# Left-over keys of a pooled attention: matmuls of 64 rows on two row halves in place of 128 rows, with a new order of issue

## The chip, the cores and the metric

One core of a Trainium2 chip. The metric is the device time of one execution in microseconds (us). The engines are TensorE (matmul, PE in the rows; its weight loads are PEld), VectorE (DVE), ScalarE (ACT), GpSimd (POOL) and SyncE (SP), which issues the DMAs.

## What is computed

Attention with pooled keys and values feeds two chained products with a normalisation between them. Batch 8, 8 heads, 576 queries, head size 64; keys and values are averaged in groups of 8, so 72 keys are left per head.

```python
k_p = k.reshape(B, H, 72, 8, D).mean(axis=3);  v_p likewise
scores = q @ k_p^T / sqrt(D);  attn = softmax(scores)
x = attn @ v_p                        # 4608 rows of 512
h = x @ w_in;  solu = h * softmax(h);  ln = layernorm(solu) * g_ln
x2 = ln @ w_out                       # 512 wide
out = ((x2 @ w1) * (x2 @ w2)) @ w3 @ w_out2
```

## The kernel before

**Split numbers.** Products that need more than one pass of the reduced float type keep a number as a high part (a rounded copy, made by ScalarE) and a low part (the difference, made by VectorE); `split` (L217 to L219) makes both. A product is then high x high, high x low and low x high.

**Units and slots.** The attention is cut into 16 groups of queries (class `Group`), two for each of the 8 batches: the even group has 256 queries, the odd one 256 and the 64 that are left over (320). While group a is in attention, the rows of earlier groups run through `h` (L753, against `w_in`) and `x` (L847 to L849, against `w_out`). Python events are laid out over time slots, 16 for each group, and build the program; behind that, `issue_order` reorders each engine's instructions by `ISSUE_ORDER`, a table in which a number skips forward or back in the engine's list and ":n" takes n of them.

**Main and left-over keys.** Of the 72 pooled keys of a head 64 are main keys and 8 are left over (KM = 64, KL = 8). For the main keys two heads share the 128 rows of a matmul: `pth` and `ptl` are the transposed probabilities' high and low parts, `VBDh` and `VBDl` the values in block-diagonal form. The left-over keys of all 8 heads, 8 x 8 = 64, are put in one tile: `normalize` writes them twice (L665), `pt` transposes them (L686) into `px`, ScalarE copies all 128 rows to `ptx` (L691), and VectorE subtracts on rows 64 to 127 (L695), so that `ptx` has the high parts on rows 0 to 63 and the low parts on rows 64 to 127. `spread_v` makes the weights for it: `vlh` (L553) holds the high left-over v on all 128 rows, masked so that a row counts for its own head only; `VLL` (L554) holds the low part on rows 0 to 63 and zeros below. `load_vl` fetches the left-over v twice, once for each 64 rows (two DMAs, L449).

**The value product.** `Group.av(i)` (L722) is called twice for each group, for the head pairs 2i and 2i + 1. For each pair five matmuls of 128 rows and 128 weight columns add up in one bank: `pth` x `VBDh`, `ptl` x `VBDh`, `pth` x `VBDl`, `ptx` x `vlh`, `ptx` x `VLL`. In even groups (256 columns) the two pairs of a call share one bank and one `split` reads both; in odd groups (320 columns) each pair has a bank, a `split` of its own and a copy-out of the 64 left-over queries (L729). Banks of the kind "ba" are three; scores (L617, two for each tile of queries) and transposed probabilities (L683) use the same three.

**At the start.** `pool_k_first` (L488) pools the first keys with matmuls whose weights have 64 columns: they write partitions 0 to 63 of a bank, then 64 to 127. L348 to L350 (the low part of `w_in`) follow on TensorE.

Of the kernel before, what the change touches and what calls it, by code (L numbers as in the profile page):

```python
# [8 lines left out]
F32 = mybir.dt.float32  # L9
# [16 lines left out]
    ),  # L26
    "Activation": (
# [20 lines left out]
    ),  # L48
    "DVE": (
# [31 lines left out]
    ),  # L81
    "Pool": (
# [9 lines left out]
    ),  # L92
# [38 lines left out]
def attention_moe_kernel(  # L131
# [286 lines left out]
    def heads(t, n):  # L418
        return t.rearrange("p (o d) -> p o d", o=1).to_broadcast([n, H, D])
# [9 lines left out]
    class Batch:  # L429
# [27 lines left out]
        def load_kl(self):  # L457
            self.load_left(KL8, k, 1)
# [1090 lines left out]
```

## Time and profile before

| | before |
|---|---|
| median of 3 runs | 1182.35 us (1180.24 to 1184.98) |
| profiled execution | 1189.81 us, of which the span from the first to the last instruction is 1188.0 us |
| granted TensorE clock, mean | 0.993 of full speed |
| busy: TensorE, VectorE | 1154.3 us (97%), 930.3 us (78%) |
| busy: ScalarE, GpSimd | 540.8 us (46%), 528.1 us (44%) |

Busy time of TensorE is that of overlapping records: a matmul's record is longer than the step to the next one, so a price of a matmul is read from starts in a timeline, and whether TensorE was held up from its waits.

### The profile page before, as it was taken

The numbers are of one execution on the slowest core, as the hardware profiler recorded it, in microseconds if no ns is written. First come the engines' busy times: TensorE is split into PE (matmuls) and PEld (weight loads), VectorE is DVE, ScalarE is ACT, GpSimd is POOL, SyncE is SP. The second block draws the span as 40 slices with busy tenths as digits, with TensorE's granted clock in tenths as the row PEclk, the third lists the DMA queues.
The fourth block names the chain that finished last, engine by engine and source line by source line (L and its number), as shares of the span: only waits on it lengthen the run. The fifth ranks groups of instructions, "written<-read, shape, count | busy, mean of one in ns | idle before, by whom it ended". The sixth has DMA issues, their size and how long they took to land.

```text
span 1188.0 us, 20236 instructions
## 1 busy us (share of the span) xinstructions
PE 1154.3 (97%) x7218; PEld 1034.6 (87%) x7218; DVE 930.3 (78%) x1376; ACT 540.8 (46%) x1399; POOL 528.1 (44%) x482
## 2 busy tenths in 40 slices
PE   7999998999999999999999999999999989999998
PEld 5788887998999999989989888888888868999998
DVE  6899898988676765686658869889785677999972
ACT  4665647575656565555422112131130145454542
POOL 2554655554232321100066757686652263555520
PEclk9999999999999999999989999999999999999999
DMA  9576586968474722355253625536441362354501
GB/s 256 139 141 150 152 208 189 238 202 209 130 174 129 172 90 90 132 190 193 81 162 115 208 94 183 187 124 195 134 142 54 118 246 72 108 184 137 177 37 72
DMA packets 167205, 178.56 MB, mean 150 GB/s; under 512 B 82624, under 2 KB 107200, under 8 KB 167104
## 3 DMA queue, kind: packets, MB, share of 16 engines
q1 hardware_dynamic: 167104, 177.26, 50.9%
q8 instruction: 57, 0.93, 0.3%
q14 instruction: 44, 0.36, 0.1%
HBM read 114.30 MB, written 62.91 MB: 149 GB/s over the span
## 4 chain that ended last, share of the span: by engine, by line
PE 78%; DVE 8%; DMA 6%; ACT 2%; SPq 2%; issue 2%; POOL 1%; ACTq 0%; DVEq 0%; POOLq 0%
PE h L753 12%; PE p L1152 10%; PE p L1154 10%; PE p L1153 10%; PE o L1392 5%; PE o L1390 5%; PE o L1391 5%; PE x L848 4%; PE x L849 4%; PE x L847 4%; PE av L722 3%; PE sc L617 2%; DMA vl<-in_v_dram 1%; PE ow L1313 1%; DMA kv<-in_k_dram 1%
## 5 line engine op out<-in xcount | busy, mean ns | idle before, releaser
L847 PE MATMUL x<-lnh,gwh 128*128 128x256 f32 x576 | 165.6, 288 | 2.3 <-ACT lnh L823 2.0
L849 PE MATMUL x<-lnh,gwl 128*128 128x256 f32 x576 | 163.6, 284 | 1.1 <-DVE gwl L376 1.0
L848 PE MATMUL x<-lnl,gwh 128*128 128x256 f32 x576 | 163.2, 283 | 0.4 <-DVE lnl L824 0.4
L847 PEld LDWEIGHTS x<-lnh,gwh 128*128 128x128 f32 x576 | 109.2, 190 | 3.6 <-ACT lnh L823 2.2
L849 PEld LDWEIGHTS x<-lnh,gwl 128*128 128x128 f32 x576 | 109.0, 189 | 1.7 <-DVE gwl L376 1.7
L848 PEld LDWEIGHTS x<-lnl,gwh 128*128 128x128 f32 x576 | 108.8, 189 | 1.5 <-DVE lnl L824 0.7
L638 ACT ACTIVATE ea<-sc,mx 128x72 f32<-128x72 f32 x320 | 98.4, 327 | 24.8 <-DVE mx L635 24.4
L658 POOL TENSOR_TENSOR pr<-ea,sm 128x512 f32<-128x512 f32 x40 | 42.5, 1062 | 141.5 <-DVE sm L654 84.1
L1168 POOL TENSOR_TENSOR a<-a,b 128x512 f32<-128x512 f32 (+1 forms) x40 | 51.5, 1286 | 109.3 <-issue 67.8
L1156 ACT ACTIVATE p<-p 128x512 f32<-128x512 f32 (+1 forms) x40 | 22.1, 552 | 163.0 <-PE p L1154 144.8
L753 PE MATMUL h<-winh,xh 128*128 128x512 f32 x288 | 94.5, 409 | 1.1 <-DVE e L768 1.1
L753 PE MATMUL h<-winl,xh 128*128 128x512 f32 x288 | 90.7, 394 | 0.0
L753 PE MATMUL h<-winh,xl 128*128 128x512 f32 x288 | 90.1, 393 | 0.0
L638 ACT ACTIVATION_READ_ACCUMULATOR ea<-sc,mx 128x1 f32 x320 | 68.3, 214 | 0.0
L762 ACT ACTIVATE e<-h,ST 128x1024 f32<-128x1024 f32 x36 | 40.2, 1116 | 57.0 <-DVE ST L761 56.7
L753 PEld LDWEIGHTS h<-winh,xl 128*128 128x128 f32 x288 | 54.0, 188 | 11.8
L753 PEld LDWEIGHTS h<-winl,xh 128*128 128x128 f32 x288 | 54.0, 188 | 11.7
L1153 PE MATMUL p<-th,w1h 128*128 128x512 f32 (+1 forms) x160 | 59.1, 370 | 0.0
L1152 PE MATMUL p<-th,w1h 128*128 128x512 f32 (+1 forms) x160 | 59.1, 369 | 0.0
L1154 PE MATMUL p<-th,w1l 128*128 128x512 f32 (+1 forms) x160 | 59.1, 369 | 0.0
L768 DVE SCALAR_TENSOR_TENSOR e<-h,e 128x1024 f32<-128x1024 f32 x36 | 44.0, 1222 | 17.5 <-ACT e L762 17.3
L753 PEld LDWEIGHTS h<-winh,xh 128*128 128x128 f32 x288 | 50.4, 191 | 7.8 <-issue 1.3
(281 smaller groups left out, 3831.5 us busy)
## 6 DMA issues: line engine op xcount, KB each, us to landing
raw<-pd SPq DMA_DIRECT2D x18, 1024.0 KB
pd<-a SPq DMA_DIRECT2D x64, 256.0 KB
ed<-turn SPq DMA_DIRECT2D x28, 512.0 KB
back<-ed SPq DMA_DIRECT2D x112, 128.0 KB
x2d<-xo SPq DMA_DIRECT2D x35, 256.0 KB
kv<-in_k_dram SPq DMA_DIRECT2D x32, 256.0 KB
kv<-in_v_dram SPq DMA_DIRECT2D x32, 256.0 KB
f<-in_moe_w_dram SPq DMA_DIRECT2D x16, 512.0 KB
```

Source lines behind the costliest of these rows:

```text
L638: nc.scalar.activation(e[0:n, x], half[a][:, h], AF.Exp, bias=mx[0:n, x : x + 1], scale=1.0, accum_out=sm[0:n, x : x + 1],)
L753: nc.tensor.matmul(self.ph[:, a], s_[:, c], w_[:, c, a * 512 : a * 512 + 512], start=first, stop=last)
L847: nc.tensor.matmul(o, gw[0][:, f, ws], self.th[:, f], start=(f == 0), stop=False)
L848: nc.tensor.matmul(o, gw[0][:, f, ws], self.tl[:, f], start=False, stop=False)
L849: nc.tensor.matmul(o, gw[1][:, f, ws], self.th[:, f], start=False, stop=(f == FC - 1))
L1152: nc.tensor.matmul(o, wh[:, c, fsl], th[:, c], start=c == 0, stop=False)
L1153: nc.tensor.matmul(o, wh[:, c, fsl], tl[:, c], start=False, stop=False)
L1154: nc.tensor.matmul(o, wl[:, c, fsl], th[:, c], start=False, stop=c == 1)
L1168: nc.gpsimd.tensor_tensor(a[:, 0], a[:, 0], b[:, 0], ALU.mult)
L1390: nc.tensor.matmul(o[:, t], h[:, c, ts], wh, start=(c == 0), stop=False)
L1391: nc.tensor.matmul(o[:, t], h[:, c, ts], wl, start=False, stop=False)
L1392: nc.tensor.matmul(o[:, t], l[:, c, ts], wh, start=False, stop=(c == 3))
```

## The change

Heads 0 to 3 of the left-over keys move to rows 0 to 63 of `ptx`, heads 4 to 7 to rows 64 to 127; in each half 32 rows hold high parts and 32 low parts (high, low, low, high from the top). `vlh` and `VLL` shrink from 8 to 4 heads of columns, since a head's row half picks it out. A call `av(i)` now works on pairs i and i + 2, one from each half, each with a bank of its own: first the three main terms of both pairs (128 rows), then `vlh` and `VLL`, each as two neighbouring matmuls of 64 rows on the two row halves. In even groups both banks are kept over both calls (columns 0 to 255 for i = 0, 256 to 511 for i = 1) and split behind the second. The low part of `ptx` now takes two VectorE instructions of 32 rows instead of one of 64, 40 more in all. `load_vl` issues three DMAs (32, 64 and 32 rows), 8 more in all. `sh` and `sl` have 128 rows, not 64. The fill of `VLL` with zeros goes, a second small mask comes. The order table is new for every engine; a gap of 352 bytes in the last stage's memory goes.

```diff
-    mask8 = const.tile([P, H], F32, tag="mask8", name="mask8")
+    masks = const.tile([P, 2, 4], F32, tag="masks", name="masks")
+    mask4, high4 = masks[:, 0], masks[:, 1]
...
-    nc.vector.tensor_tensor(mask8, m16[:, 0:8], m16[:, 8:16], ALU.add)
+    nc.vector.tensor_reduce(mask4, m16.rearrange("p (t i) -> p i t", i=4), axis=AX.X, op=ALU.add)
+    nc.vector.tensor_tensor(high4, m16[:, 0:4], m16[:, 12:16], ALU.add)
...
-    VLL = A1.tile([P, H, D], F32R, tag="VLL", name="VLL")
-    nc.gpsimd.memset(VLL.bitcast(F32), 0.0)
+    VLL = A1.tile([P, 4, D], F32R, tag="VLL", name="VLL")
...
-            self.load_left(self.vn, v, 2)
+            self.load_left(self.vn, v, ((0, 4, 0), (0, H, 32), (4, 4, 96)))
...
-            self.vlh = A.tile([P, H, D], F32R, tag="vlh", name=f"vlh{self.b}", bufs=1)
-            nc.gpsimd.tensor_tensor(self.vlh, heads(self.vn[:, 0:D], P), head_mask(P), ALU.mult)
-            nc.gpsimd.tensor_tensor(VLL[0:64], heads(sl, 64), head_mask(64), ALU.mult)
+            sh = A.tile([P, D], F32R, tag="sh", name=f"sh{self.b}", bufs=1)
+            sl = A.tile([P, D], F32, tag="sl", name=f"sl{self.b}", bufs=1)
+            split(sh, sl, self.vn[:, 0:D])
+            self.vlh = A.tile([P, 4, D], F32R, tag="vlh", name=f"vlh{self.b}", bufs=1)
+            nc.gpsimd.tensor_tensor(self.vlh, heads(self.vn[:, 0:D]), head_mask(mask4), ALU.mult)
+            nc.gpsimd.tensor_tensor(VLL, heads(sl), head_mask(high4), ALU.mult)
...
+            left = pr[0:n, H * KM :].rearrange("p (a s x) -> p a s x", a=2, s=2)
             for c in range(2):
                 nc.gpsimd.tensor_tensor(
-                    pr[0:n, (H + c) * KM : (H + c) * KM + KM].rearrange("p (h k) -> p h k", h=H),
-                    e[0:n, :, KM:KP],
-                    s8.to_broadcast([n, H, KL]),
+                    left[:, :, c].rearrange("p a (h k) -> p a h k", k=KL),
+                    e[0:n, :, KM:KP].rearrange("p (a h) k -> p a h k", a=2),
+                    s8.rearrange("p (a h) o -> p a h o", a=2).to_broadcast([n, 2, 4, KL]),
                     ALU.mult,
                 )
...
-                nc.vector.tensor_tensor(x[64:P], px[64:P], x[64:P].bitcast(F32), ALU.subtract)
+                for r in (32, 64):
+                    nc.vector.tensor_tensor(x[r : r + 32], px[r : r + 32], x[r : r + 32].bitcast(F32), ALU.subtract)
...
-            for p in (2 * i, 2 * i + 1):
-                if self.g or p % 2 == 0:
-                    av_bank = bank(f"av{self.a}_{p}")
...
+            if self.g or i == 0:
+                self.ab = [bank(f"av{self.a}_{i}_{a}") for a in range(2)]
+            off = 0 if self.g else i * U
+            av = [t[:, off : off + w] for t in self.ab]
+            for a in range(2):
+                p = 2 * a + i
+                vh, vl = [t[:, p].rearrange("p a d -> p (a d)") for t in (VBDh, VBDl)]
+                for n, (l, r) in enumerate(((vh, self.pth), (vh, self.ptl), (vl, self.pth))):
+                    nc.tensor.matmul(av[a], l, r[:, p, 0:w], start=(n == 0), stop=False)
+            for l in (bt.vlh, VLL):
+                for a in range(2):
+                    ks = slice(64 * a, 64 * a + 64)
+                    vp = l[ks, 2 * i : 2 * i + 2].rearrange("p j d -> p (j d)")
+                    nc.tensor.matmul(av[a], vp, self.ptx[ks, 0:w], start=False, stop=l is VLL)
+            for a in range(2):
+                c = 2 * a + i
+                if self.g:
+                    split(x[0][:, c], x[1][:, c], av[a][:, 0:U])
...
+                elif i:
+                    cs = slice(2 * a, 2 * a + 2)
+                    split(x[0][:, cs], x[1][:, cs], self.ab[a].rearrange("p (c n) -> p c n", c=2))
...
-    gap(RB, 352)
```

In the new list of TensorE, one group with 256 columns and its surroundings read, written out (F: a main term of 128 rows; H: a matmul of 64 rows):

```
x (12 matmuls of another unit), F F F F F F, H H H H, scores of the next tile (first half), h x 8, scores (second half), h ...
```

## Rows read from the trace of the kernel before

**Rows 1.** The page: span, busy time, and the chain that ended last by engine.

```profile
span 1188.0 us, 20236 instructions
...
PE 1154.3 (97%) x7218; PEld 1034.6 (87%) x7218; DVE 930.3 (78%) x1376; ACT 540.8 (46%) x1399; POOL 528.1 (44%) x482
...
PE 78%; DVE 8%; DMA 6%; ACT 2%; SPq 2%; issue 2%; POOL 1%; ACTq 0%; DVEq 0%; POOLq 0%
```

**Rows 2.** Busy time of each engine in two stages of the attention.

```profile
core 0: us, PE busy (x) PEld busy (x) DVE busy (x) ACT busy (x) POOL busy (x), PEclk, DMA share, GB/s
50.00:250.00 200.00, 191.72 (x1246) 172.19 (x1245) 179.18 (x330) 127.51 (x459) 109.16 (x143) 0.99 0.72 176
250.00:510.00 260.00, 258.46 (x1747) 238.75 (x1747) 183.53 (x325) 158.84 (x531) 78.07 (x114) 1.00 0.53 148
```

**Rows 3.** All waits of TensorE's matmuls, 250 to 510 us: total, times, longest.

```profile
PE pt L683 <- POOL pr L658: 1.5, 3, 1.0
```

**Rows 4.** Left-over terms of `av`, L722: ns min/median/max, first and last start, forms.

```profile
L722 PE MATMUL av<-ptx,vlh x64: 274/297/468, 43.8 to 498.2; 128*128 128x256 f32 x32, 128*128 128x320 f32 x32
L722 PE MATMUL av<-ptx,VLL x64: 278/304/468, 45.0 to 498.4; 128*128 128x256 f32 x32, 128*128 128x320 f32 x32
```

**Rows 5.** Timeline of TensorE around three calls of `av`: start us, us, instructions.

```profile
401.10 0.27 PE L722 MATMUL av<-pth,VBDh 128*128 128x256 f32 x1
...
402.28 0.28 PE L847 MATMUL x<-lnh,gwh 128*128 128x256 f32 x1
...
404.89 1.14 PE L617 MATMUL sc<-bdt,qT 128*128 128x144 f32 x8
406.34 0.62 PE L753 MATMUL h<-winl,xh 128*128 128x512 f32 x2
406.80 0.63 PE L753 MATMUL h<-winh,xl 128*128 128x512 f32 x2
...
437.38 0.31 PE L722 MATMUL av<-pth,VBDh 128*128 128x320 f32 x1
...
438.84 0.62 PE L753 MATMUL h<-winh,xh 128*128 128x512 f32 x2
```

**Rows 6.** Timeline of TensorE while the first keys are pooled (64 weight columns).

```profile
10.52 0.82 PE L488 MATMUL pkm<-ident,kv 128*64 128x128 f32 x9
...
13.25 0.82 PE L488 MATMUL pkm<-ident,kv 128*64 128x128 f32 x6
```

**Rows 7.** Timeline where the pooling ends, with VectorE and the weight loads.

```profile
12.91 0.83 DVE L338 SCALAR_TENSOR_TENSOR cvb<-f,cvb 128x512 int32<-128x512 int32 x1
...
14.00 0.30 PEld L348 LDWEIGHTS w<-cvb,ident 128*128 128x128 f32 x2 [0.17 <-issue]
```

**Rows 8.** VectorE's subtraction on `ptx`: all of it, and from 50 to 250 us.

```profile
L695 DVE TENSOR_TENSOR ptx<-px,ptx x40: 227/294/296, 29.9 to 488.2; 64x128 fp32r<-64x128 f32 x32, 64x64 fp32r<-64x64 f32 x8
...
50.00:250.00 200.00, 4.81 (x17) 0.99 0.72 176
```

**Rows 9.** Timeline of ScalarE and VectorE behind two calls of `av`.

```profile
404.87 1.04 ACT L823 ACTIVATE lnh<-back 128x1024 fp32r<-128x1024 f32 x1
405.82 0.58 ACT L218 ACTIVATE xh<-av 128x512 fp32r<-128x512 f32 x1
406.51 0.68 DVE L219 TENSOR_TENSOR xl<-av,xh 128x512 fp32r<-128x512 f32 x1
...
438.31 0.38 ACT L218 ACTIVATE xh<-av 128x256 fp32r<-128x256 f32 x1 [0.81 <-PE av L722]
438.72 0.42 DVE L219 TENSOR_TENSOR xl<-av,xh 128x256 fp32r<-128x256 f32 x1 [0.71 <-ACT xh L218]
439.06 0.22 DVE L729 COPY X<-av 128x64 f32<-128x64 f32 x1
```

**Rows 10.** GpSimd's product into `vlh` and the DMAs of the left-over v.

```profile
L553 POOL TENSOR_TENSOR vlh<-vl,mask x8: 1042/1042/1373, 38.5 to 441.8; 128x512 fp32r<-128x512 f32 x8
...
L449 SPq DMA_DIRECT2D vl<-in_v_dram x16: 614/628/644, 19.6 to 387.4; - x16
```

More of the change, by code (lines that the diff above doesn't have):

```diff
@@ L416, in attention_moe_kernel, with heads, head_mask @@
     nc.gpsimd.memset(KL8[64:P, 2 * D : 4 * D], 0.0)
-    def heads(t, n):
-        return t.rearrange("p (o d) -> p o d", o=1).to_broadcast([n, H, D])
-    def head_mask(n):
-        return mask8[0:n].rearrange("p (h o) -> p h o", o=1).to_broadcast([n, H, D])
+    def heads(t):
+        return t.rearrange("p (o d) -> p o d", o=1).to_broadcast([P, 4, D])
+    def head_mask(t):
+        return t.rearrange("p (h o) -> p h o", o=1).to_broadcast([P, 4, D])
     def tree(t, n):
@@ L445, in load_main, with load_left @@
             to[i] = t
-        def load_left(self, t, src, copies):
-            for c in range(copies):
+        def load_left(self, t, src, places):
+            for h, n, r in places:
                 nc.sync.dma_start(
-                    t[64 * c : 64 * c + 64], src[self.b, :, 512:S, :].rearrange("h (k e) d -> h k (e d)", e=POOL)
+                    t[r : r + 8 * n], src[self.b, h : h + n, 512:S, :].rearrange("h (k e) d -> h k (e d)", e=POOL)
                 )
@@ L457, in load_kl @@
         def load_kl(self):
-            self.load_left(KL8, k, 1)
+            self.load_left(KL8, k, ((0, H, 0),))
         def load_v(self, i):
@@ L547, in spread_v @@
         def spread_v(self):
-            sh = A.tile([64, D], F32R, tag="sh", name=f"sh{self.b}", bufs=1)
-            sl = A.tile([64, D], F32, tag="sl", name=f"sl{self.b}", bufs=1)
-            nc.scalar.activation(sh, self.vn[0:64, 0:D], AF.Copy)
-            nc.vector.tensor_tensor(sl, self.vn[0:64, 0:D], sh.bitcast(F32), ALU.subtract)
-            self.vlh = A.tile([P, H, D], F32R, tag="vlh", name=f"vlh{self.b}", bufs=1)
-            nc.gpsimd.tensor_tensor(self.vlh, heads(self.vn[:, 0:D], P), head_mask(P), ALU.mult)
-            nc.gpsimd.tensor_tensor(VLL[0:64], heads(sl, 64), head_mask(64), ALU.mult)
+            sh = A.tile([P, D], F32R, tag="sh", name=f"sh{self.b}", bufs=1)
[4 more added lines that the diff above has]
+            nc.gpsimd.tensor_tensor(VLL, heads(sl), head_mask(high4), ALU.mult)
     class Group:
@@ L706, in av @@
             x = X[self.a]
-            for p in (2 * i, 2 * i + 1):
-                if self.g or p % 2 == 0:
-                    av_bank = bank(f"av{self.a}_{p}")
-                av = av_bank if self.g else av_bank[:, p % 2 * U : p % 2 * U + U]
-                pair = lambda t: t[:, 2 * p : 2 * p + 2].rearrange("p a d -> p (a d)")
-                vhp = VBDh[:, p].rearrange("p a d -> p (a d)")
-                vlp = VBDl[:, p].rearrange("p a d -> p (a d)")
-                terms = [
-                    (vhp, self.pth[:, p, 0:w]),
-                    (vhp, self.ptl[:, p, 0:w]),
-                    (vlp, self.pth[:, p, 0:w]),
-                    (pair(bt.vlh), self.ptx[:, 0:w]),
-                    (pair(VLL), self.ptx[:, 0:w]),
-                ]
-                for n, (l, r) in enumerate(terms):
-                    nc.tensor.matmul(av[:, 0:w], l, r, start=(n == 0), stop=(n == 4))
-                if self.g == 0 and p % 2:
-                    ps = slice(p - 1, p + 1)
-                    split(x[0][:, ps], x[1][:, ps], av_bank.rearrange("p (c n) -> p c n", c=2))
-                elif self.g == 1:
-                    split(x[0][:, p], x[1][:, p], av[:, 0:U])
-                    left = X8[bt.b // 4][:, p].rearrange("p (g s b) -> p g b s", g=2, b=2)[:, bt.b % 4 // 2, bt.b % 2]
-                    nc.vector.tensor_copy(left, av[:, U : U + TL])
@@ new lines, in av @@
+            for l in (bt.vlh, VLL):
[7 more added lines that the diff above has]
+                    split(x[0][:, c], x[1][:, c], av[a][:, 0:U])
+                    left = X8[bt.b // 4][:, c].rearrange("p (g s b) -> p g b s", g=2, b=2)[:, bt.b % 4 // 2, bt.b % 2]
+                    nc.vector.tensor_copy(left, av[a][:, U : U + TL])
+                elif i:
+                    cs = slice(2 * a, 2 * a + 2)
+                    split(x[0][:, cs], x[1][:, cs], self.ab[a].rearrange("p (c n) -> p c n", c=2))
```

165 rows, old and new, of the table ISSUE_ORDER are left out of this document.

## The prediction

> **What bounds the kernel now.** I read the page first: TensorE is busy for 97% of the span, the next engine, VectorE, for 78%, and the chain that ended last runs over TensorE for 78% of its length [rows 1]. Those are averages over unlike stages, so the second view is the busy time by stage. The change lies in the attention part, which sends the products concerned between 44 and 498 us [rows 4]. In the late half of it, 250 to 510 us, TensorE is busy for 258.46 of 260 us and VectorE for 183.53; in the early half, 50 to 250 us, TensorE has 191.72 of 200 us and VectorE 179.18 [rows 2]. The reader is to see two regimes: late, TensorE alone sets the pace, and a microsecond on it is a microsecond of the span; early, TensorE still leads but VectorE is close behind. The third view, TensorE's waits, bears that out: from 250 to 510 us its matmuls waited for others 1.5 us in all [rows 3]. So the change is worth what it does to TensorE's own time in `av`, and everything else costs only where it makes TensorE wait.
>
> **What a matmul of `av` costs now.** The records (median 0.30 us [rows 4]) overlap one another; the price is the step from one start to the next. With 256 columns ten matmuls go from 401.10 to 402.28 us, 0.118 each; with 320 columns ten go from 437.38 to 438.84 us, 0.146 each [rows 5]. The terms of the left-over keys (`vlh` and `VLL`) are 64 matmuls each, half of them of either width [rows 4]: 64 x 0.118 + 64 x 0.146 = 16.9 us.
>
> **The saving.** After the change these 128 matmuls use 64 rows each, two neighbours on different row halves and into different banks. If two such neighbours run side by side, each pair costs one step instead of two. I wrote out TensorE's new list from the order table: 60 of the 64 pairs stand side by side (31 with 256 columns, 29 with 320; the order splits the others). Saved at most 31 x 0.118 + 29 x 0.146 = 7.9 us. No matmul of before uses 64 rows, so whether pairs run side by side is read from the nearest thing: the pooling of k at the start, whose matmuls fill one half of the columns (form 128*64). Six in a row on one half take 0.82 us, (0.82 - 0.27) / 5 = 0.11 us a step; where the two halves meet, nine take the same 0.82 us, 0.069 a step on average [rows 6]. So two halves of the array do work at once, at no loss of rate of either; I take the same for row halves.
>
> **The price of going between whole and halved array.** The same place has the only change from halved to whole in the trace. The last of the six column-half matmuls starts at 13.25 + 5 x 0.11 = 13.80 us. The next, L348, uses the whole array; its operand had been done at 12.91 + 0.83 = 13.74 us. Yet its weight load starts only at 14.00, after an idle time that the view puts down to nothing it can see ("issue"), and the second load follows 0.11 us behind the first (0.30 us for two of 0.19), so the first matmul can stream from 14.11 [rows 7]. From the last half matmul to the first whole one are 0.31 us instead of one step of 0.11: 0.20 us lost, 0.09 until the load may start and 0.11 for a load that elsewhere hides behind the matmul ahead of it. In the TensorE list after the change the 64-row matmuls form 36 runs (28 of them of four), each with a matmul of 128 rows before and behind it: 72 changes. The way in isn't in the trace; its bounds are 0 and the 0.20 of the way out, or anything below if it hides. I take 0.20, since the array has the same reason to empty itself in both directions: 72 x 0.20 = 14.4 us, between 0 and 14.4. The Trainium skill, TensorEngine Tiling (Array Packing), section Tiling Modes, says the same of the cause: a change of tiling mode drains TensorE, one of the tile alone doesn't. The trace agrees for one change, with the 0.20 us above.
>
> Net on TensorE: 14.4 - 7.9 = +6.5 us. For one run of four at 256 columns: 4 x 0.118 = 0.47 us before; after, 0.20 in, 2 x 0.118, 0.20 out, 0.64 us.
>
> **VectorE.** The subtraction on the left-over probabilities, one instruction on rows 64 to 127, becomes two, on rows 32 to 63 and 64 to 95. Its length goes with the columns, so a second one costs what the first does: 0.294 us at 128 columns, 40 calls, 11 us in all, 4.81 us in the early half (17 calls) [rows 8]. Late, VectorE has 76 us free: nothing. Early it has 21 of 200 us free: between 0 and 4.8; I take 1 us, because TensorE leads there too.
>
> **Banks.** `av` now takes two of the three "ba" banks at once. For groups without left-over queries both halves stay in their banks until the second call is through, so the second half of the next scores must wait for a split. The new order allows for that: the two score matmuls are moved behind eight matmuls of `h`. The cover is four score records of 0.12 us, (1.14 - 0.27) / 7, and eight of `h` of 0.23, 0.46 for two, some 2.3 us after the last `av`; the split of the second bank ended 406.51 + 0.68 - 404.89 = 2.3 us after it before [rows 5, 9]. Even, then: 0 to 1 us (one more ScalarE copy of 1.04 us ahead [rows 9]) in each of eight batches. I take 0.5 in all. Where `av` splits two columns of one bank, the copies move later by up to five matmuls, 0.7 us; the bank is asked for 1.8 us after the call's end (six `h` matmuls and three of the next `av`), and copy, subtraction and copy-out take 0.38 + 0.42 + 0.22 us: nothing.
>
> **What is hidden.** The two spreading products on GpSimd halve (1.04 us for the one, eight times [rows 10], the other has as many columns): some 8 us of an engine that is busy for 44% [rows 1], worth nothing on the path. The rearranged writes of the small probabilities (L665) keep their count and size. The copy and the subtraction that make `sh` and `sl` keep their columns. The left-over v comes in three DMAs instead of two: SyncE's queue issues one in 0.63 us [rows 10], and what is queued behind (q, k and v of the next batch, the spills) goes out 0.63 us later, eight times; TensorE waited for no DMA in the late half [rows 3]. If that cover were gone: at most 8 x 0.63 = 5 us. One fill on GpSimd less and one small VectorE instruction more, once each at the start of the program, I take at nothing. The new tables of the other engines follow these edits; in the steady part the TensorE list is the old one but for `av` and those scores.
>
> **Sum.** +6.5 + 1 + 0.5 = +8.0 us. The profiled execution took 1189.81 us (span 1188.0 [rows 1] and 1.8 around it), 7.5 us over the median of the timed runs; it would become 1197.8. Carried to the median: 1182.35 + 8.0 = 1190.35 us.
>
> **Rivals.**
> 1. *No emptying between whole and row-halved array*: 0.20 was paid by column halves and may belong to them. Then -7.9 + 1.5 = -6.4 us, 1176 us. For it: a row half touches no other row's operand. Against it: the load in rows 7 stood still with its data ready. The Trainium skill, TensorE: Matmul & The Clock Gate, Part 3, prices a packed set as one matmul and about 4 ns for each further tile, with no change of mode in the sum; 60 pairs at that would save 7.6 us. No row here has a packed set of row tiles. It decides below a change of 7.9 / 72 = 0.11 us. Chance 0.25, with partial prices in it.
> 2. *Only the way out costs*: 36 x 0.20 - 7.9 + 1.5 = +0.8 us, 1183 us. For it: only that way is seen. Chance 0.12.
> 3. *Loads of the two row halves go one after the other, or the halves don't run side by side at all* (the change doesn't do what it says). In rows 6 a load had 64 columns, so two still fitted a step; here each has 128, 0.11 us [rows 7]. One by one, a run of four lasts 0.09 + 4 x 0.11 + 0.12 + 0.20 = 0.85 us for 0.47 at 256 columns, 0.88 for 0.58 at 320: 16 x (0.38 + 0.30) = +11, with the 1.5 about +12.5, 1195 us. Without any overlap: 14.4 + 1.5, 1198 us. Chance 0.15.
>
> **How the numbers follow.** My forecast (both ways paid, pairs side by side) has 0.48, at 1190.35 us, its own range 1186 to 1195. Cases faster than before by more than 0.5% (5.9 us, about what a measurement of this kernel can tell from no change): the better part of rival 1, 0.15. Within 0.5%: the rest of rival 1 (0.10), rival 2 (0.12), the lower edge of the forecast where the way in is cheaper (0.11): 0.33. Slower by more: 0.52. The range takes in rival 1 to its middle and rival 3 to its upper bound: 1177 to 1198.
>
> **What will show it.** In a timeline of TensorE around an `av` in the late half: the two `vlh` matmuls starting within a few hundredths of each other (pairs), a gap of 0.3 us between the last matmul of 128 rows and the first of 64, and again behind the last of 64 (the changes). A run of four that takes 0.64 us from its first gap to its last is my forecast; 0.24 us rival 1; 0.85 us rival 3. VectorE's `ptx` group should have 80 instructions of 0.29 us, and TensorE's waits in the late half stay under 5 us. I am wrong if the run is shorter than 0.47 us, or if the time moves while the runs don't: then it is the order, not the matmuls.

## The result and the profile after

The changed kernel takes 1193.24 us (median of 4, 1191.01 to 1194.17) beside 1183.66 us for the kernel before on the same chip; the ratio is 1.0070, 95% interval 1.0050 to 1.0090. Two more comparisons of the same pair, further down, gave 1.0073 (1.0049 to 1.0097) and 1.0068 (1.0048 to 1.0087). Together that is +8.3 us, give or take 1.4; the forecast was +8.0 us, 1190.35 us. The profiled execution has a span of 1192.4 us.

The page: span, busy time by engine, and the chain that ended last, as in [rows 1].

```profile
span 1192.4 us, 20295 instructions
...
PE 1158.0 (97%) x7218; PEld 1026.6 (86%) x7218; DVE 927.4 (78%) x1417; ACT 544.0 (46%) x1399; POOL 515.9 (43%) x481
...
PE 82%; DVE 6%; DMA 4%; ACT 3%; SPq 2%; issue 2%; POOL 1%; ACTq 0%; DVEq 0%; POOLq 0%
```

TensorE still sets the pace, with as many matmuls as before. VectorE has 41 instructions more (40 of them the second subtractions), GpSimd 12 us less.

The same two stages as in [rows 2], and TensorE's waits of the late one, as in [rows 3].

```profile
core 0: us, PE busy (x) PEld busy (x) DVE busy (x) ACT busy (x) POOL busy (x), PEclk, DMA share, GB/s
50.00:250.00 200.00, 194.46 (x1263) 171.20 (x1262) 177.15 (x342) 126.94 (x455) 100.61 (x139) 0.99 0.66 169
250.00:510.00 260.00, 258.32 (x1722) 231.96 (x1721) 191.65 (x352) 159.91 (x534) 77.01 (x118) 1.00 0.56 154
```

```profile
engine line waited for: us in total, times, longest us
PE pt L685 <- POOL pr L659: 1.1, 2, 0.9
PE sc L618 <- DVE xl L222: 0.6, 2, 0.3
```

In the late half TensorE runs fewer matmuls in the same 260 us (1722 for 1747) and waits no more than before (1.7 us for 1.5): it needs longer for its own work. The one new wait, scores on `xl`, is the bank term of the sum.

The new matmuls (forms, as in [rows 4]), the subtraction on `ptx` and the spreading product (as in [rows 8, 10]):

```profile
L723 PE MATMUL av<-ptx,vlh x64: 379/397/413, 42.8 to 498.8; 64*128 64x256 f32 x32, 64*128 64x320 f32 x32
L723 PE MATMUL av<-ptx,VLL x64: 275/301/410, 43.5 to 499.0; 64*128 64x256 f32 x32, 64*128 64x320 f32 x32
```

```profile
L698 DVE TENSOR_TENSOR ptx<-px,ptx x80: 216/283/290, 29.1 to 489.1; 32x128 fp32r<-32x128 f32 x64, 32x64 fp32r<-32x64 f32 x16
```

```profile
L554 POOL TENSOR_TENSOR vlh<-vl,masks x8: 613/614/672, 38.4 to 441.9; 128x256 fp32r<-128x256 f32 x8
```

Half the rows save the subtraction nothing: 283 ns for 32 rows, 294 for 64 [rows 8].

One run of four with 256 columns, matmuls and then weight loads (start us, us), to set beside the ten even steps of [rows 5]:

```profile
459.89 0.28 PE L718 MATMUL av<-pth,VBDh 128*128 128x256 f32 x1
460.01 0.28 PE L718 MATMUL av<-ptl,VBDh 128*128 128x256 f32 x1
460.13 0.28 PE L718 MATMUL av<-pth,VBDl 128*128 128x256 f32 x1
460.34 0.39 PE L723 MATMUL av<-ptx,vlh 64*128 64x256 f32 x2
460.56 0.28 PE L723 MATMUL av<-ptx,VLL 64*128 64x256 f32 x2
460.77 0.39 PE L850 MATMUL x<-lnh,gwh 128*128 128x256 f32 x1
461.00 0.28 PE L851 MATMUL x<-lnl,gwh 128*128 128x256 f32 x1
```

```profile
460.01 0.19 PEld L718 LDWEIGHTS av<-pth,VBDl 128*128 128x128 f32 x1
460.34 0.19 PEld L723 LDWEIGHTS av<-ptx,vlh 64*128 64x128 f32 x2
460.44 0.19 PEld L723 LDWEIGHTS av<-ptx,VLL 64*128 64x128 f32 x2
460.77 0.19 PEld L850 LDWEIGHTS x<-lnh,gwh 128*128 128x128 f32 x1
460.88 0.19 PEld L851 LDWEIGHTS x<-lnl,gwh 128*128 128x128 f32 x1
```

The reader is to see four things. The two matmuls of a pair stand in one row with x2: they start within 0.01 us, and so do their two weight loads. The 64-row matmul starts 0.21 us behind the last of 128 rows, where the step is 0.12. The first of 128 rows behind it starts 0.21 us after the last pair, and the one after that 0.23 later, because its load couldn't run ahead: the load at 460.77 starts with its own matmul, that of the next 0.11 later. From the last main term to the second `x` are 0.87 us; six steps of 0.118 were 0.71. The run costs 0.16 us. With 320 columns the same distance is 0.95 us for 0.85: 0.10.

```profile
381.32 0.31 PE L718 MATMUL av<-pth,VBDl 128*128 128x320 f32 x1
...
382.28 0.28 PE L851 MATMUL x<-lnl,gwh 128*128 128x256 f32 x1
```

At the end of the attention part the trace has waits that [rows 3] do not reach to, for they end at 510 us. TensorE's waits from 555 to 580 us in the kernel after, then TensorE and ScalarE there:

```profile
PE x L850 <- ACT lnh L826: 2.2, 1, 2.2
PE x L851 <- DVE lnl L827: 0.9, 1, 0.9
```

```profile
566.32 0.61 PE L756 MATMUL h<-winh,xl 128*128 128x512 f32 x2
569.12 0.38 PE L850 MATMUL x<-lnh,gwh 128*128 128x256 f32 x1 [2.19 <-ACT lnh L826]
570.38 0.58 PE L851 MATMUL x<-lnl,gwh 128*128 128x256 f32 x1 [0.88 <-DVE lnl L827]
```

```profile
566.98 1.15 ACT L221 ACTIVATE w1h<-raw 128x512 fp32r<-128x512 f32 x2 [3.93 <-PE h L756]
568.03 1.04 ACT L826 ACTIVATE lnh<-back 128x1024 fp32r<-128x1024 f32 x1
```

The second `lnh` copy of unit 16 stands behind two copies into `w1h`, which belong to the last stage and wait 3.93 us for the last `h`. So TensorE's `x` waits 2.2 us for `lnh` and 0.9 for `lnl`. In the kernel before, both `lnh` copies stand ahead of all `w1h`:

```profile
563.42 1.05 ACT L823 ACTIVATE lnh<-back 128x1024 fp32r<-128x1024 f32 x1
567.47 3.76 ACT L218 ACTIVATE w1h<-raw 128x512 fp32r<-128x512 f32 x7 [3.00 <-PE h L753]
```

Behind the idle time of the kernel after, the granted clock goes to the lower of its two levels:

```profile
569.00:571.00 2.00, 1.00 (x4) 0.80 (x5) 1.89 (x3) 2.00 (x5) 0.00 (x0) 0.63 0.68 226
571.00:573.00 2.00, 2.00 (x11) 2.00 (x11) 2.00 (x3) 1.49 (x4) 0.00 (x0) 0.50 0.58 176
573.00:576.00 3.00, 3.00 (x16) 3.00 (x16) 3.00 (x6) 1.26 (x3) 1.92 (x2) 0.50 0.56 174
```

The total came out where the forecast put it. Whether it came from where the forecast put it is what the experiments are for.

### The profile page after: what moved, and what is told of

Read it like the earlier page. It is cut to its first block, busy times and chain, and to the rows that moved or that the text cites. A ratio compares the mean times of both kernels' runs of the same rounds, so it can differ in the third digit from the quotient of the medians.

```text
span 1192.4 us, 20295 instructions
## 1 busy us (share of the span) xinstructions
PE 1158.0 (97%) x7218; PEld 1026.6 (86%) x7218; DVE 927.4 (78%) x1417; ACT 544.0 (46%) x1399; POOL 515.9 (43%) x481
## 4 chain that ended last, share of the span: by engine, by line
PE 82%; DVE 6%; DMA 4%; ACT 3%; SPq 2%; issue 2%; POOL 1%; ACTq 0%; DVEq 0%; POOLq 0%
PE h L756 14%; PE p L1155 9%; PE p L1156 9%; PE p L1157 9%; PE x L850 5%; PE x L851 5%; PE o L1394 5%; PE x L852 5%; PE o L1395 5%; PE o L1393 5%; PE sc L618 3%; PE av L718 2%; DMA qb<-in_q_dram 1%; PE ow L1316 1%; PE ow L1314 1%
## 5 line engine op out<-in xcount | busy, mean ns | idle before, releaser
L850 PE MATMUL x<-lnh,gwh 128*128 128x256 f32 x576 | 168.0, 292 | 3.6 <-ACT lnh L826 3.6
```

Of the source, the lines that this page charges most:

```text
L850: nc.tensor.matmul(o, gw[0][:, f, ws], self.th[:, f], start=(f == 0), stop=False)
```

## The experiments

Two theories of the +8.3 us. A (the prediction): nearly all of it is TensorE's price for the 36 runs of 64-row matmuls. B: a good part is the new order of issue, above all the place of `lnh` at the end of the attention part. "Lag" below is how much later the same matmul (the n-th `h`, the n-th `p`) starts than in the kernel before, taken from the starts in two traces.

**The change again, twice** (no edit), as e0 and, on another chip, e11.

> The change itself, unaltered, beside the others on the same chip. Before plus 6 to 11 us (it was 0.7% slower, interval 0.5 to 0.9%).

> The change itself once more, on the same chip as the other three of this call, so that they can be set against it: 7 to 9 us over the kernel before.

Measured: 1192.06 us, ratio 1.0073; and 1191.82 us, ratio 1.0068 (intervals above). Both traces have the waits of 2.2 and 0.9 us at the end.

**The kernel before, profiled again.**

> The kernel before, profiled once more, as a trace to set the others against. In its first profile TensorE reaches the same matmul at 213 us some 3 us later than in the trace with the two subtractions alone, and no work there explains it. Theory: that was the one execution; this trace has the same steps of av (0.118 and 0.146 us) and its left-over terms no runs with gaps, but its span is nearer to 1182 than to 1188 us. Rival: the 3 us belong to the kernel before and show again.

Measured: 1185.86 us, span 1184.1. It stands nearer to the timed median than the first profile, so lags are taken against it. Behind 510 us, where [rows 3] end, TensorE's timeline shows two waits:

```profile
513.58 0.70 PE L753 MATMUL h<-winh,xh 128*128 128x512 f32 x2 [0.32 <-DVE e L768]
526.41 0.70 PE L753 MATMUL h<-winh,xh 128*128 128x512 f32 x2 [1.11 <-DVE e L768]
```

The kernel after waits for nothing there, and the change's lag falls by 2.1 us from 502 to 526 us in both e0 and e11. That isn't because it comes there late. The first profile of the kernel before reaches 502 us 2.4 us later than this one and still waits 1.1 us:

```profile
PE h L753 <- DVE e L768: 1.1, 1, 1.1
```

The kernel with whole rows and the tail mended (e9, below) comes 0.9 us earlier than this one and waits for nothing. All four profiles with the old order have the wait (0.6 to 1.4 us in all), none of the ten with the new order has it, so it goes with the order, or with another edit that those ten share.

**What a run costs**: in groups 8 to 15 the run of four is split by one main term, 16 runs and 32 changes of the array more (`m` are the six main terms in the order in which they were issued, `v` and `l` the matmuls on `vlh` and `VLL`, 0 and 1 the row half).

```diff
...
+            m = [(main, a, n) for a in range(2) for n in range(3)]
+            v0, v1, l0, l1 = [(half, a, l) for l in (bt.vlh, VLL) for a in range(2)]
+            if self.a >= 8:
+                todo = m[:5] + [v0, v1, m[5], l0, l1]
+            else:
+                todo = m + [v0, v1, l0, l1]
...
```

> The change with the price doubled in 16 of 32 calls (groups 8 to 15): the last main term of 128 rows stands between the pair of vlh and the pair of VLL, so each of these calls has two runs of 64-row matmuls instead of one, 32 changes of the array more; nothing is added or left out. Theory: 16 x 0.40 = 6.4 us more than the change, before plus 14 to 18 us. Rival (the changes are hidden, or cost only where the weights are late): the change plus 0 to 2 us.

Measured: 1197.29 us, ratio 1.0114 (1.0079 to 1.0149), +13.5 us on the kernel before (9.3 to 17.6), just under the 14 to 18 expected, and 5.2 us over e0 by the medians (the ratios leave 0 to 10). One such call in the trace:

```profile
405.18 0.28 PE L718 MATMUL av<-ptl,VBDh 128*128 128x256 f32 x1
405.39 0.39 PE L723 MATMUL av<-ptx,vlh 64*128 64x256 f32 x2
405.70 0.39 PE L718 MATMUL av<-pth,VBDl 128*128 128x256 f32 x1
406.02 0.39 PE L723 MATMUL av<-ptx,VLL 64*128 64x256 f32 x2
406.34 0.76 PE L618 MATMUL sc<-bdt,qT 128*128 128x144 f32 x4
```

Every step between the two kinds is 0.21 or 0.31 to 0.32 us: 0.21 where the load had been hidden, 0.31 where the array changes twice in a row. A call lasts 0.39 us longer, 0.20 for each change; 16 x 0.39 = 6.2 us.

**The same in the early half**, in groups 0 and 2 to 6: 12 runs more (the diff is to the kernel above). The reason: the change's lag in the early half (47 to 240 us) rises by only +1.5, -0.7 and +2.1 us in its three profiles. Part of their spread is the clock: from 190 to 205 us the granted clock is 0.89 in the two others and in e2, and 1.00 in e0, the one with -0.7.

```diff
-            if self.a >= 8:
+            if self.a in (0, 2, 3, 4, 5, 6):
                 todo = m[:5] + [v0, v1, m[5], l0, l1]
```

> The change with the run of four 64-row matmuls split in two (one main term of 128 rows between the pairs) in six groups of the early half, 0, 2, 3, 4, 5 and 6: 12 runs and 24 changes between whole and halved array more, nothing else. In the late half the same edit in eight groups cost 5.2 us for 16 runs, with 0.39 us more of each call in the trace. Theory (early, TensorE has room to give, because what feeds it sets the pace, so the price of a run is mostly hidden there, and that is why the early half of the change shows no loss): 0 to 2 us over the change, though each call is 0.39 us longer in the trace here too. Rival (TensorE sets the pace early as well, as the prediction took it): 12 x 0.39 = 4.7 us over the change.

Measured: 1195.99 us, ratio 1.0098 (1.0082 to 1.0115), 4.2 us over the change on the same chip (e11) by the medians, 3.6 (0.5 to 6.7) by the ratios. That is near the rival's figure, 4.7; the theory that the early half hides most of the price is the less likely one, though its upper end, 2, lies in the interval. The lag of this kernel rises by 6.6 us from 47 to 240 us (an estimated 1.7 of it because its granted clock is 0.77, not 0.89, over the 15 us from 190 to 205 us), and a split call is 0.39 us longer here too.

**The subtractions alone**: the kernel before with its one subtraction on 64 rows made in two of 32.

```diff
-                nc.vector.tensor_tensor(x[64:P], px[64:P], x[64:P].bitcast(F32), ALU.subtract)
+                for r in (64, 96):
+                    nc.vector.tensor_tensor(x[r : r + 32], px[r : r + 32], x[r : r + 32].bitcast(F32), ALU.subtract)
```

> The kernel before with one part of the change alone: the low part of ptx made by two VectorE instructions of 32 rows (64 to 95, 96 to 127), the second right behind the first; 40 instructions more, all else as before. Theory: 11 us more of VectorE's work, nearly all of it beside TensorE: before plus 0 to 2 us. Rival (VectorE's extra work is on the path in the early half): before plus 4 to 5 us or more.

Measured: 1186.24 us, ratio 1.0024 (1.0007 to 1.0041): +2.8 us, 0.8 to 4.9, between the theory's 0 to 2 and the rival's 4 to 5. The forecast's 1 us lies in the interval, at its lower end.

**The tail of the order mended**: the change with `lnh` and `lnl` of unit 16 ahead of the two `w1h` and `w1l`.

```diff
         assert len(order) == len(traced)
+        if engine == "Activation":
+            order[723:726] = [order[i] for i in (725, 723, 724)]
+        elif engine == "DVE":
+            order[779:782] = [order[i] for i in (781, 779, 780)]
```

> The change with two entries of the order tables put back as before had them: at the end of the attention rows' work ScalarE makes the second part of lnh of unit 16 ahead of the two copies w1h, and VectorE its lnl ahead of the two w1l. In the change lnh stood behind w1h, which waits for the last product h, and TensorE's x waited 2.2 us for lnh and 0.9 us for lnl, after which the granted clock was 0.50 for some 5 us. Theory (the tail of the order table cost what the lag shows there, -0.5 to -1.3 us before it and +3.6 to +5.1 behind it): 4.5 to 6 us faster than the change, about 1187.5, +3 to +4 us on the kernel before; TensorE's waits for lnh gone and the clock at 1.00 from 566 to 576 us. Rival (the tail's loss is made good later, as another wait or as a part of the stage behind it that waits for weights anyway): no more than 1 us, about 1192.

Measured: 1188.19 us, ratio 1.0032 (1.0020 to 1.0043), +3.8 us on the kernel before. Against the change (1.0070 over its three comparisons, 1.0012 either way) that is 4.5 us less, 2.5 to 6.5. ScalarE and the granted clock there:

```profile
561.76 1.05 ACT L830 ACTIVATE lnh<-back 128x1024 fp32r<-128x1024 f32 x1
565.80 3.76 ACT L225 ACTIVATE w1h<-raw 128x512 fp32r<-128x512 f32 x7 [2.99 <-PE h L760]
```

```profile
571.00:573.00 2.00, 2.00 (x19) 2.00 (x18) 1.49 (x3) 1.39 (x3) 0.13 (x1) 1.00 0.84 259
573.00:576.00 3.00, 3.00 (x27) 3.00 (x27) 3.00 (x4) 1.73 (x3) 2.78 (x2) 1.00 0.12 44
```

TensorE ran 19 matmuls in the 2 us where the change had 11. About half of the +8.3 us was three neighbouring entries in each of two lists, which have nothing to do with 64 rows. Theory B holds, in this part.

**The tail of the kernel before spoilt** in the same way, its matmuls untouched.

```diff
+        if engine == "Activation":
+            order[723:726] = [order[i] for i in (724, 725, 723)]
+        elif engine == "DVE":
+            order[739:747] = [order[i] for i in (746, 740, 739, 741, 742, 743, 744, 745)]
```

> The kernel before with only the tail of its order spoilt in the same way: ScalarE's second lnh of unit 16 behind two w1h, VectorE's lnl likewise. The matmuls stay as they are. Theory (the tail alone costs what it showed in the change): 4 to 6 us slower than before, about 1188, with the waits of x for lnh and the granted clock at 0.50 behind them. Rival (it cost there only together with the other edits): within 1.5 us of before.

Measured: 1187.21 us, ratio 1.0012 (0.9999 to 1.0024): +1.4 us, at most 2.8. That is the rival's range; the 4 to 6 us of the theory didn't come. The waits come up as foreseen (2.2 and 0.9 us) and the clock falls:

```profile
566.00:569.00 3.00, 3.00 (x14) 3.00 (x15) 3.00 (x5) 1.37 (x4) 0.00 (x0) 0.51 0.68 238
```

The lag rises by 5.1 us from 549 to 591 us, and 3.1 us of it are given back by 608: there, in e2, VectorE waits 3.6 us for a DMA that writes `x2d` (this holds up `b`, and TensorE's `p` 2.7 us behind that), and in this kernel neither wait is there. In the changed kernel both are still there behind the stall (3.7 and 2.7 us in e0). So the same fault costs about 5 us of TensorE's time at its place in either kernel; how much of it stays in the total is settled behind it, 1.4 us here and 4.5 in the change. Why the DMA came in time here and not in the change is open.

**Whole rows again, masks moved**: the change with its left-over terms on 128 rows, masked weights of 8 heads, with the masks moved out of the constants' memory.

```diff
-    masks = const.tile([P, 2, 4], F32, tag="masks", name="masks")
+    masks = A1.tile([P, 2, H], F32, tag="masks", name="masks")
...
-                    vp = l[ks, 2 * i : 2 * i + 2].rearrange("p j d -> p (j d)")
-                    nc.tensor.matmul(av[a], vp, self.ptx[ks, 0:w], start=False, stop=l is VLL)
+                    vp = l[:, 2 * p : 2 * p + 2].rearrange("p j d -> p (j d)")
+                    nc.tensor.matmul(av[a], vp, self.ptx[:, 0:w], start=False, stop=l is VLL)
```

> The change with one part undone: the left-over terms use all 128 rows again (vlh and VLL have 8 heads of columns, zeros in the other row half), so no matmul of 64 rows and no pairs are left; the order table, two banks, two subtractions and three DMAs stay. Theory (72 changes between whole and halved array at 0.20 us, less 7.9 us of pairs): it gives back 6.5 us, so before plus 1 to 4 us, and a call of av takes ten steps of 0.118 or 0.146 us without a gap. Rival (the new order, the banks and VectorE carry the loss): it stays at before plus 7 to 10 us.

Measured: 1202.32 us, ratio 1.0161 (1.0136 to 1.0186), ten us slower than the change in place of six faster, outside theory and rival. The steps of `av` are back, but the lag grows by 6.7 us from 621 to 916 us, in stage `p`, which the edit doesn't touch. TensorE from 650 to 900 us in this kernel, then in the next one:

```profile
650.00:900.00 250.00, 250.00 (x1080) 1.00 0.46 153
```

```profile
650.00:900.00 250.00, 250.00 (x1104) 1.00 0.47 154
```

1080 matmuls for 1104, at a full clock and no wait: 0.2315 us each for 0.2264. Taking the masks (32 bytes) out of the constants moves what is allocated behind them; apart from that the two kernels differ by two small VectorE instructions at the start.

**Whole rows, everything in its place**: `masks` stays where it is, the wider masks lie elsewhere.

```diff
+    masks8 = A1.tile([P, 2, H], F32, tag="masks8", name="masks8")
...
-    VLL = A1.tile([P, 4, D], F32R, tag="VLL", name="VLL")
+    VLL = A1.tile([P, H, D], F32R, tag="VLL", name="VLL")
```

> The change with the left-over terms on 128 rows again, 64 weight columns groups masked to their own head as in the kernel before, everything else of the change kept (two banks, two subtractions, three DMAs, the order tables), and this time with every tile of the constants at its place, which the earlier kernel with whole rows had moved by 32 bytes. It costs two GpSimd products of twice the columns and three small VectorE instructions at the start. Theory (36 runs with 0.40 us of changes each against 60 steps saved are +6.5 us of TensorE, and the 32 bytes were why the earlier one gave 1202): 4 to 6.5 us faster than the change, 1186 to 1189, the steps of av at 0.118 and 0.146 throughout, and stage p at the pace of before. Rival 1 (most of the price of the runs was covered by VectorE, which sets the pace early): 0 to 3 us faster. Rival 2 (it was not the place but the whole rows): again some 10 us slower than the change.

Measured: 1191.33 us, ratio 1.0055 (1.0036 to 1.0074). Stage `p` is at the old pace, so rival 2 falls. But the kernel is only 1.8 us faster than the change (0.9 slower to 4.5 faster), which is rival 1's range.

**Whole rows and the tail mended**, both edits.

> The change with the left-over terms on 128 rows and its constants in their places, and with lnh and lnl of unit 16 ahead of w1h and w1l as well. Theory (the two causes add): the 6.5 us that whole rows alone stood over before, less the 4.8 that the order of the copies gave: +1 to +3 us on the kernel before, what is left being the second subtractions (2.8 us by themselves) and GpSimd's probabilities, for which the late half waits 1.2 us more with products of full width. Rival (the two hide one another, both filling the same slack in front of the last stage): +4 to +6 us.

Measured: 1186.43 us, ratio 1.0010 (0.9997 to 1.0023): the two causes add. The mended tail gives 5.3 us here (2.6 to 8.1, against e8). It is level with the kernel before, and 2.6 us (0.6 to 4.7) faster than the change with the tail mended. With the pair above, whole rows give back some 2.3 us in the new order, 0.7 to 3.9 (the two differences weighted by their intervals), not the 6.2 that the runs take on TensorE. Part of the difference shows in its waits from 250 to 510 us:

```profile
PE pt L696 <- POOL pr L670: 2.7, 2, 1.4
PE sc L629 <- DVE xl L226: 0.8, 1, 0.8
```

TensorE waits 2.7 us for the probabilities, 1.6 more than with 64 rows (1.1 with the tail mended). If that is due to GpSimd's spreading products, at full width in an order made for half of it, the runs' price is some 3.9 us, 2.3 to 5.5, and about 2 us remain that these runs don't place. But a TensorE that has less to do also comes earlier and so waits longer; the runs don't separate the two.

**The halves apart**: in groups 8 to 15 both matmuls of one half are issued first, then both of the other (the diff is to the kernel with the split runs).

```diff
             if self.a >= 8:
-                todo = m[:5] + [v0, v1, m[5], l0, l1]
+                todo = m + [v0, l0, v1, l1]
```

> The change with the four 64-row matmuls of a call in another order in groups 8 to 15: both of one row half, then both of the other (first half vlh, VLL, then second half vlh, VLL), so that only the two in the middle are neighbours on different halves. No change of array more or less. If only neighbours run side by side, a run has three steps instead of two: 16 x 0.13 = +2.1 us on the change, and the trace shows the second and third start together; if nothing runs side by side unless paired with its own kind, four steps, +4.2 us. If a half that is free takes its matmul whenever it comes, no change: 0.

Measured: 1193.13 us, ratio 1.0081 (1.0060 to 1.0103), 1.3 us over e11 by the medians; the ratios leave -2 to +5, so the time decides nothing. The trace does:

```profile
406.14 0.28 PE L718 MATMUL av<-pth,VBDl 128*128 128x256 f32 x1
406.36 0.39 PE L723 MATMUL av<-ptx,vlh 64*128 64x256 f32 x2
406.58 0.28 PE L723 MATMUL av<-ptx,VLL 64*128 64x256 f32 x2
406.79 0.39 PE L859 MATMUL x<-lnh,gwh 128*128 128x256 f32 x1
```

Issued as `vlh`, `VLL`, `vlh`, `VLL`, they start as `vlh`, `vlh` (within 0.01 us), `VLL`, `VLL`: the other half's matmul starts ahead of one that was issued before it. So it is in all 16 calls: the second `vlh` starts 6 to 7 ns behind the first, where the runs of four in groups 0 to 7, whose order is unaltered, have 3 to 4. The third case holds, at the same 0.64 us from the last main term to the next matmul of 128 rows.

## Why the prediction was right, and where it was right by luck

The time lay 2.9 us from the forecast (1.3 of them because the kernel before took 1183.66 us beside it, not 1182.35), and the step on which the rivals hung was right. But the forecast put all +8.0 us into the attention part, and only +3.8 (2.4 to 5.1) are there: that is the change with the tail mended. Two errors of 4 to 5 us cancelled.

- **Pairs side by side**: right. Two neighbours start within 0.01 us and their loads as well; rival 3 (loads one after the other) is out. The Trainium skill, TensorE: Matmul & The Clock Gate, Part 3, has about 4 ns for each further tile; the trace agrees (the second of the pair at 460.34 starts 4 ns behind the first).
- **0.20 us for a change, both ways**: right, and more evenly than argued. The run of four takes 0.63 us from where the first step should have ended (forecast 0.64; rivals 0.24 and 0.85), the way in is 0.21 us for a step of 0.12, and splitting a run in two cost 0.39 each in the trace. Rivals 1 and 2 are out. Only the sign "a gap of 0.3 us" isn't there as such: the gaps are 0.21 us on either side, and the 0.11 of the load stands in the step behind each. So it is in the trace of the kernel before as well: at the place of [rows 7] L348's first matmul starts at 14.00 us, with its load, and not at the 14.11 that the prediction took. The Trainium skill, TensorEngine Tiling (Array Packing), Tiling Modes, names the drain without a figure; here it is 0.09 us at each change, with 0.11 for a load that can't run ahead.
- **TensorE's sum, +6.5**: right as a count. 14 runs of four at 0.157, 14 at 0.104 and the eight that the order splits, 0.22 to 0.39 each and 2.5 together, make 6.2 us. What fails is the step from there to the span: whole rows give back only 2.3 (0.7 to 3.9), or some 3.9 if the longer wait for the probabilities is charged to GpSimd's wider products.
- **VectorE, +1**: probably too small, though the interval holds it. By itself the second subtraction costs 2.8 us (0.8 to 4.9). Late I had put it at nothing for the 76 us that VectorE has free, and there the lag of this kernel grows by 1.2 us from 240 to 502 us, where the two other profiles with the old order differ from e2 by 0.3 either way.
- **Banks, +0.5**: right in size. The new wait of scores for `xl` is 0.6, 1.9 and 0.2 us in the three profiles of the change. The third DMA, at nothing, was right too as far as TensorE's waits show: from 250 to 510 us none is for a DMA.
- **"The new tables ... in the steady part the TensorE list is the old one"**: here the prediction failed, twice. I had written out TensorE's list and not ScalarE's and VectorE's, and nothing outside the steady part. The end of their lists holds the price of 4.5 us (2.5 to 6.5; in the kernel before the same fault cost 1.4), which the forecast has at nothing. Written out, the entry of `lnh` behind `w1h` is plain in the table, and so is its wait for the last `h`.
- **The wait at 513 and 526 us**: not in the sum at all, for the rows ended at 510 us. The old order waits there 0.6 to 1.4 us, the new one never, whether it comes there late or early: a gain that the forecast has at nothing.

The ledger, then: runs 6.2 and subtractions 2.8 are 9.0 us; +3.8 (2.4 to 5.1) were measured with the tail mended. Some 5 us are missing. The wait at 513 and 526 us that is gone makes 0.6 to 1.4 of them. The rest is missing in the early half above all, where the three profiles of the change lag by 1 us on average (another execution of one and the same kernel can lie 3 us off there), though the early split runs cost 3.6 of their 4.7. The likeliest owner is the new order itself, which would then have gained elsewhere what it lost at its tail: with whole rows, two subtractions and the mended tail it stands 1.2 us over the kernel before, where the subtractions alone stand 2.8 over it. That difference, 1.7 us, give or take 2.5, isn't clear of zero, and no run has the new order with all the old work, so this is argued, not shown.

## What to carry to other kernels

Going from 128 rows to 64 and back costs 0.20 us each way here, so a run of pairs has to save more than 0.40 us: at 0.118 us a step that is four pairs side by side (three at 0.146), and a run of two pairs loses. Where an order is made anew, write out every engine's list to its end, not only the bounding engine's and not only the steady part: an instruction that waits long, moved ahead of one that is due, holds that one up (here 3.1 us of waits on TensorE, and 1.4 or 4.5 us of the total by what follows). And a total that agrees with the forecast shows little about its terms; mend or spoil each by itself before you believe them.

## What the hardware showed that I had not expected

- **A place in memory sets the pace of matmuls.** 32 bytes less ahead of stage `p`'s operands, and its matmuls went from 0.2264 to 0.2315 us a step (2.3%) at a granted clock of 1.00 and without a wait, 6.7 us over the stage. Which operand it is wasn't tried. An experiment that takes out a tile has to leave its place filled.
- **A short stall can cost more than itself.** 3.1 us of waits within 4 us were followed by a granted clock of 0.50 from 571 to 576 us, and 16 matmuls in 3 us where 27 run at 1.00. All seven profiles with these two waits and the matmuls of 64 rows or of the kernel before show the lower clock behind them, and none of the five without the waits has it there. It isn't certain to come: the two kernels with whole rows and the same waits had the clock at 1.00 behind them, and the lag of the second rose by 3.6 us up to 591 us in place of 5 to 6 (by 608 us it had lost 6.3, at the waits that open the last stage). Why these two kept it is open.
- **The row halves aren't held to the order of issue between them.** A half that is free starts its own matmul ahead of an earlier one of the other half, in 16 of 16 calls of that experiment, 6 to 7 ns behind the first.
